# K slots in bundles of two, R's low channels in K's row-tile stretch: a convolution followed by a channel mix on one core

## The chip, the cores and the metric

The kernel runs on one core of a Trainium2 chip, alone. The metric is the device time of one execution in microseconds (us), the median of several runs. The engines are PE (TensorE, matmuls), PEld (its weight loads, which run beside the matmuls), DVE (VectorE), ACT (ScalarE), POOL (GpSimd) and SP (SyncE, which here only issues DMAs). PSUM, where matmuls write, has 8 banks of 512 float32 per partition.

## What is computed

Batch 8, sequence 4160, 192 channels, float32 in and out. First a causal convolution of 7 taps, with one softmaxed filter for each of 8 heads of 24 channels; then a channel mix on its result `y`:

```python
y  = conv(x, softmax(weight))                 # taps 0..6 back in time, per head
y1 = y shifted one step back in time
xk = mu_k * y + (1 - mu_k) * y1
xr = mu_r * y + (1 - mu_r) * y1
k  = relu(xk @ w_k)                           # 192 -> 1024
v  = (k * k) @ w_v                            # 1024 -> 192
out = sigmoid(xr @ w_r) * v                   # w_r: 192 x 192
```

## The kernel before

The work goes by **pairs** of batch rows ("sequences"), four in all. A pair is cut into **steps** of 512 positions (the first pair has 256, seven times 512, 256), and a tail of 64. A step of 512 has 8 **slots**; a slot is 128 of the 1024 K channels for both sequences, written to a PSUM tile of two banks (`psK`, two such tiles). 192 channels do not fit the 128 rows of the array, so each product over them is split: the *high* part contracts 128 channels, the *low* part the other 64. The low channels of sequence 0 lie on partitions 0 to 63 and those of sequence 1 on 64 to 127 (`xk[:, 2]`, `xr[:, 2]`), and K's low part is done as two matmuls of 64 rows (two row tiles), one for each half (`k_mm`, L343). Two slots form a bundle, in which PE does high, low, low, high: one stretch in row tiles for two slots.

After K: `k_relu` (ACT, L372) takes PSUM to `k_sb`, `k_square` (DVE, L391) squares it into `k2`. `v_mm` (PE, L433) makes 128 positions of one sequence from 8 matmuls over `k2`; `r_mm` makes the same 128 positions of R from a matmul over the high channels (L415) and one of the low channels (L416). L416 uses all 128 rows: the weights `wr[:, 2:4]` are padded with zeros where the other sequence's low channels lie. `r_sig` (ACT, L423) and `v_out` (DVE, L446) take two such tiles at once, and SP writes them out (L451).

Ahead of this runs the convolution. x is loaded by POOL's DMAs in **groups** of up to 10 blocks of 112 positions (`load_x`, L103 to L109, three buffers `xb`); `conv_mm` (PE, L199) multiplies by a banded matrix `toe`, in chunks of one to three heads; `conv_out` (ACT, L219 and L222) copies to `y`. `y` must then be transposed to have channels on partitions (`yT`). The first four groups do that on PE (`tr_mm` L257, `tr_out` on DVE L268); the others go through DRAM: `y_write` and `y_read`, a transposing DMA, both on SP (L234, L242). `diff` (DVE, L281) and `mix` (DVE, L301; four calls a step, for xk and xr, high channels 1024 wide and low channels 512 wide) make xk and xr from `yT`.

The order on each engine is the order in which the code calls: it is written out by hand. Tables `early`, `pe`, `act`, `dve` say which calls stand at which slot, relative to the first slot n0 of a step: `diff` at n0-7, the mixes at n0-5 to n0-2 (closer to the step for the first ones), R two slots ahead of its V, V from two slots after the step's last slot, `y_read` 17 slots (8.5 bundles) ahead of the step that needs it (11 slots in one group), the loads 14 slots before the group's convolution. A transposed pair of blocks is copied out one slot after its transposes. PSUM: `psK` 4 banks, `psV` 2 (V's results), `psM` 2 single banks, shared by convolution, transposes and R.

Of the kernel before, what the change touches and what calls it, by code (L numbers as in the profile page):

```python
# [14 lines left out]
def kernel(  # L15
# [29 lines left out]
    WARM = 34  # L45
# [7 lines left out]
    psM = ctx.enter_context(tc.tile_pool(name="psM", bufs=2, space=bass.MemoryType.PSUM))  # L53
# [4 lines left out]
    slots = []  # L58
    first_step = {}
    for p in range(NPAIR):  # L60
# [3 lines left out]
        for L in sizes + [TAIL]:  # L64
            ns = L * NF // STEP if L > TAIL else 1
            steps.append((p, t0, L, len(slots), ns))
            slots += [(len(steps) - 1, j) for j in range(ns)]
            t0 += L
    NSLOT = len(slots)
# [3 lines left out]
    for p in range(NPAIR):  # L73
        blk0 = 0
        for nb, s, on_pe in (
            ((3, 0, True), (4, 1, True), (5, 2, True), (4, 3, True), (10, 4, False), (6, 6, False), (6, 7, False))
# [59 lines left out]
    wr = const.tile([P, 4, D], BF16)  # L136
# [9 lines left out]
    def load_wr():  # L146
        nc.gpsimd.dma_start(out=wr[:, 0, :], in_=moe_w_r[0:P, :])
        for i in (1, 2):
            nc.gpsimd.dma_start(out=wr[0:LO, i, :], in_=moe_w_r[P:D, :])
        for i in (1, 3):  # L150
            nc.gpsimd.dma_start(out=wr[LO:P, i, :], in_=moe_w_r[P:D, :])
# [32 lines left out]
    ys, yTs, y_drams = {}, {}, {}  # L184
    conv_ps = {}
# [5 lines left out]
    def conv_mm(g, c, pool=None, tag="m"):  # L191
# [4 lines left out]
        ps = (pool or psM).tile([P, nb, 2, G * len(hs)], FP32, tag=tag, name="ps_c")  # L196
# [52 lines left out]
    def tr_mm(g, j):  # L249
# [3 lines left out]
        ps = psM.tile([P, 3, 2, BLK], BF16, tag="m", name="ps_t")  # L253
# [21 lines left out]
    def diff(s):  # L275
        p, t0, L, _, _ = steps[s]
        c0 = YC + t0
        d = two.tile([P, 3, STEP], BF16, tag="diff", name="d")
# [9 lines left out]
    def mix(s, i, part):  # L288
# [4 lines left out]
        if part == 0 and L > TAIL:  # L293
# [30 lines left out]
    def k_mm(n):  # L324


        s, j = slots[n]
        p, _, L, _, _ = steps[s]
        if L == TAIL:
            return k_mm_tail(n, p)  # L330
        xk = xks[s]
        ps = psK.tile([P, 2, BANK], FP32, tag="k", name="ps_k")
        k_ps[n] = ps
        first = j % 2 == 0
        nf = STEP // L


        def go(hi, start):
            for f in range(nf):
                fs = slice((j * nf + f) * P, (j * nf + f + 1) * P)  # L340
                for i in range(2):
                    r = slice(0, P) if hi else slice(i * LO, (i + 1) * LO)
                    nc.tensor.matmul(  # L343
                        out=ps[:, i, f * L : (f + 1) * L],
# [240 lines left out]
    with tc.manual_schedule():  # L585
# [4 lines left out]
        for ns in bundles():  # L590
            for n in ns:
                run(early, n)
# [41 lines left out]
```

## Time and profile before

| | |
|---|---|
| median of 3 runs | 469.6 us (469.21 to 470.67) |
| the profiled execution | 468.94 us, of which the span of the profile is 467.2 and 1.74 lie around it |
| granted PE clock, mean | 0.99 |
| PE busy | 445.2 us, 95% of the span |
| DVE busy | 390.4 us, 84% |
| ACT busy | 374.6 us, 80% |
| DMA | 65.79 MB, 141 GB/s on average |

The span runs from the first to the last instruction. A busy share is a mean over all stages, so it says which engine may be the bound, not that it is the bound everywhere; that is read from the timeline of each stage, and from which wait ends last there. Matmuls overlap in the pipeline: the duration of one (246 ns for 192 columns) is longer than the distance from one start to the next, and it is the distance that costs time.

### The profile page before, as it was taken

How to read it: one execution, taken by the hardware profiler on the slowest of the kernel's cores; microseconds unless marked ns; L12 is line 12 of the kernel's file. 1: busy time of each engine (PE TensorE's matmuls, PEld its weight loads, DVE VectorE, ACT ScalarE, POOL GpSimd, SP SyncE). 2: the span in 40 equal slices, each digit the busy share in tenths (PEclk: the TensorE clock that was granted, in tenths of full speed). 3: DMA queues.
4: the chain of work that ended last, by engine and by line, in shares of the span. 5: the costliest groups of instructions: out<-in, count | busy, mean ns of one | idle time of the engine just before them, and what ended most of it. 6: DMA issues, size and time to landing. Idle time of an engine off the chain costs nothing.

```text
span 467.2 us, 9868 instructions
## 1 busy us (share of the span) xinstructions
PE 445.2 (95%) x3892; PEld 300.6 (64%) x3954; DVE 390.4 (84%) x616; ACT 374.6 (80%) x549; POOL 51.1 (11%) x71
## 2 busy tenths in 40 slices
PE   7788999999999999999999999999999999999996
PEld 3454766666776666666676666666676666666676
DVE  2778988797998879889798989978898987999873
ACT  2489888988879797888879788888978888777771
POOL 5812211000010041000002041000002000000000
PEclk9799999999999999999999999999999999999999
DMA  7996699972459599945367679937157753511222
GB/s 89 160 174 106 162 197 156 233 200 68 127 142 183 148 139 229 181 129 139 93 173 119 165 133 214 229 100 187 52 152 138 173 135 100 153 65 56 69 69 94
DMA packets 138942, 65.79 MB, mean 141 GB/s; under 512 B 89936, under 2 KB 138464, under 8 KB 138896
## 3 DMA queue, kind: packets, MB, share of 16 engines
q1 hardware_dynamic: 98000, 49.26, 41.0%
q0 software_dynamic: 40896, 15.90, 30.0%
q8 instruction: 31, 0.51, 0.4%
q14 instruction: 15, 0.12, 0.1%
HBM read 31.59 MB, written 37.52 MB: 148 GB/s over the span
## 4 chain that ended last, share of the span: by engine, by line
PE 91%; ACT 2%; issue 2%; DMA 2%; DVE 1%; DVEq 0%; ACTq 0%
PE ps_k L343 38%; PE ps_v L433 37%; PE ps_c L199 5%; PE ps_r L416 5%; PE ps_r L415 5%; ACT k_sb L372 1%; DMA w_scr<-w_row 1%; PE ps_k L360 1%; DMA toe<-w_scr 1%; ACT y L219 1%; DMA w_raw<-in_weight_dram 1%; PE ps_t L257 1%; DVE yT L268 0%; ACT y L222 0%; DVE k L391 0%
## 5 line engine op out<-in xcount | busy, mean ns | idle before, releaser
L372 ACT ACTIVATE k_sb<-ps_k 128x1024 bf16<-128x1024 f32 x260 | 260.2, 1026 | 35.8 <-PE ps_k L343 31.8
L343 PE MATMUL ps_k<-xk,wk 64*128 64x512 bf16 (+2 forms) x994 | 206.0, 376 | 9.5 <-ACT k_sb L372 0.9
L433 PE MATMUL ps_v<-wv,k 128*128 128x192 bf16 x2048 | 210.8, 246 | 0.0
L433 PEld LDWEIGHTS <-k 128*128 128x128 bf16 x2048 | 175.4, 98 | 30.6 <-issue 1.4
L391 DVE TENSOR_TENSOR k<-k_sb 128x1024 bf16<-128x1024 bf16 x256 | 174.8, 684 | 16.7 <-ACT k_sb L372 16.0
L343 PEld LDWEIGHTS <-wk 64*128 64x128 bf16 (+1 forms) x1056 | 56.2, 96 | 109.2 <-issue 107.9
L446 DVE TENSOR_TENSOR o_sb<-ps_v,r_sb 128x384 f32<-128x384 f32 x132 | 72.2, 547 | 39.6 <-PE ps_v L433 34.7
L423 ACT ACTIVATE r_sb<-ps_r 128x384 bf16<-128x384 f32 x132 | 64.3, 487 | 38.1 <-PE ps_r L416 37.3
L301 DVE SCALAR_TENSOR_TENSOR xr<-d,mu,yT 128x1024 bf16<-128x1024 bf16 (+1 forms) x66 | 65.1, 988 | 0.1
L301 DVE SCALAR_TENSOR_TENSOR xk<-d,mu,yT 128x1024 bf16<-128x1024 bf16 (+1 forms) x66 | 64.4, 977 | 0.2
L415 PE MATMUL ps_r<-wr,xr 128*128 128x192 bf16 x256 | 62.8, 246 | 0.0
L416 PE MATMUL ps_r<-wr,xr 128*128 128x192 bf16 x256 | 62.8, 246 | 0.0
L219 ACT CAST y<-ps_c 112x480 bf16<-112x480 f32 (+4 forms) x100 | 47.9, 483 | 10.4 <-PE ps_c L199 10.2
L199 PE MATMUL ps_c<-xb,toe 128*112 128x480 bf16 (+5 forms) x152 | 46.2, 332 | 5.3 <-DMA toe<-w_scr 2.9
L109 POOL DMA_DIRECT2D xb<-in_x_dram x38 | 34.9, 928 | 26.8 <-PE ps_c L199 15.9
L281 DVE TENSOR_TENSOR d<-yT 128x1536 bf16<-128x1536 bf16 (+2 forms) x37 | 31.8, 859 | 0.4 <-DMA yT<-y_dram 0.2
L108 POOL DMA_DIRECT2D xb<-in_x_dram x8 | 4.3, 538 | 215.7 <-PE ps_k L343 206.3
L199 PEld LDWEIGHTS <-toe 128*112 128x112 bf16 x152 | 19.2, 134 | 12.1 <-DMA toe<-w_scr 3.4
L222 ACT CAST y<-ps_c 112x480 bf16<-112x480 f32 (+8 forms) x53 | 25.2, 482 | 0.2 <-DVE yT L227 0.2
L415 PEld LDWEIGHTS <-xr 128*128 128x128 bf16 x256 | 25.0, 98 | 0.0
L416 PEld LDWEIGHTS <-xr 128*128 128x128 bf16 x256 | 25.0, 98 | 0.0
L103 POOL DMA_DIRECT2D xb<-in_x_dram x8 | 4.6, 581 | 62.4 <-PE ps_r L416 61.0
(46 smaller groups left out, 67.8 us busy)
## 6 DMA issues: line engine op xcount, KB each, us to landing
out_dram<-o_sb SPq DMA_DIRECT2D x128, 192.0 KB, 2.3
y_dram<-y SPq DMA_DIRECT2D x7, 840.0 KB, 5.0
xb<-in_x_dram POOLq DMA_DIRECT2D x12, 432.0 KB, 12.0
y_dram<-y SPq DMA_DIRECT2D x6, 756.0 KB, 4.6
xb<-in_x_dram POOLq DMA_DIRECT2D x8, 480.0 KB, 13.2
xb<-in_x_dram POOLq DMA_DIRECT2D x6, 384.0 KB, 6.6
y_dram<-y SPq DMA_DIRECT2D x2, 504.0 KB, 10.7
xb<-in_x_dram POOLq DMA_DIRECT2D x4, 240.0 KB, 5.3
```

Source lines behind the costliest of these rows:

```text
L109: nc.gpsimd.dma_start(out=xb[:, lo:hi, s, :], in_=bass.AP(tensor=x.tensor, offset=x.offset + (b * S + t0 + lo * BLK) * D, ap=[[D, P], [BLK ...
L199: nc.tensor.matmul(out=ps[:BLK, :, :, i * G : (i + 1) * G], lhsT=toe[:, h, :], rhs=xbs[g][:, :nb, :, h * G : (h + 1) * G], start=True, sto ...
L219: copy(out=yh[:, :, :, c0 : c0 + n], in_=ps[:BLK, :, :, 0:n])
L301: nc.vector.scalar_tensor_tensor(out=o, in0=d[r0:r1, sl, :L], scalar=mu[r0:r1, i, part : part + 1], in1=yT[r0:r1, sl, c0 : c0 + L], op0=AL ...
L343: nc.tensor.matmul(out=ps[:, i, f * L : (f + 1) * L], lhsT=wk[r, 0 if hi else 1, fs], rhs=xk[r, i if hi else 2, :L], start=start and f == ...
L372: nc.scalar.activation(out=k_sb, in_=ps.rearrange("p a b -> p (a b)"), func=AF.Relu)
L391: nc.vector.tensor_tensor(out=o, in0=i, in1=i, op=ALU.mult)
L415: nc.tensor.matmul(out=o, lhsT=hi, rhs=wr[:, 0, :], start=True, stop=False)
L416: nc.tensor.matmul(out=o, lhsT=lo, rhs=wlo, start=False, stop=True)
L423: nc.scalar.activation(out=r_sb[:, :n, :], in_=ps[:, :n, :], func=AF.Sigmoid)
L433: nc.tensor.matmul(out=o, lhsT=k2[:, f, t * P : (t + 1) * P], rhs=wv[:, f, :], start=(f == 0), stop=(f == NF - 1),)
L446: nc.vector.tensor_tensor(out=o_sb[:, :n, :], in0=v_ps.pop(m)[:, :n, :], in1=r_sbs.pop(m)[:, :n, :], op=ALU.mult)
```

## The change

- A **bundle** is now the unit of every table: two K slots, and one V/R tile, which is 128 positions of *both* sequences. V's tile of a step starts in the bundle right behind the step's last one (before: one bundle further on).
- R's low part is done as K's: two matmuls of 64 rows, one for each sequence, in the same row-tile stretch as the two low parts of K. `wr` shrinks to two parts and its zeros go. R's PSUM tile takes two banks, one for each sequence, so `psM` is now one tile of two banks (`bufs=1`), which R and the convolution use in turn. Two convolution chunks can share the tile, a bank each.
- Transposes on PE now take `psV`'s banks, up to three behind each other in one bundle, each with its copy.
- In the first pair the groups are 3, 4, 5, 4, 5, 5 on PE and 5, 5, 2 through DRAM (before: 3, 4, 5, 4 on PE, and 10, 6, 6 through DRAM).
- The order within a bundle is fixed by the loop at the end. `diff` stands 5 bundles ahead of its step and the mixes at 4, 3, 2 and 1 (three buffers for `diff`); x is loaded 4 bundles before its convolution, `y_read` stands 3 bundles before the `diff` that needs it (2 in the first pair).
- 46 warm-up matmuls instead of 34.

```diff
-    WARM = 34
+    WARM = 46
-    psM = ctx.enter_context(tc.tile_pool(name="psM", bufs=2, space=bass.MemoryType.PSUM))
+    psM = ctx.enter_context(tc.tile_pool(name="psM", bufs=1, space=bass.MemoryType.PSUM))
...
+    tiles = []
+    for s, (p, t0, L, b0, nb) in enumerate(steps):
+        for c in range(max(1, L // P)):
+            tiles.append((s, c, max(b0 + nb, tiles[-1][2] + 1) if tiles else b0 + nb))
...
-            ((3, 0, True), (4, 1, True), (5, 2, True), (4, 3, True), (10, 4, False), (6, 6, False), (6, 7, False))
+            ((3, 0, True), (4, 1, True), (5, 2, True), (4, 3, True), (5, 4, True), (5, 5, True), (5, 6, False), (5, 7, False), (2, 8, False))
...
+    def m_banks():
+        shared[:] = [psM.tile([P, 2, BANK], FP32, tag="m", name="ps_m"), 2]
+        return shared[0]
+    def m_bank():
+        if shared[1] != 1:
+            m_banks()
+            shared[1] = 0
+        shared[1] += 1
+        return shared[0][:, shared[1] - 1, :]
...
-        ps = psM.tile([P, 3, 2, BLK], BF16, tag="m", name="ps_t")
+        ps = psV.tile([P, 3, 2, BLK], BF16, tag="v", name="ps_t")
...
-        d = two.tile([P, 3, STEP], BF16, tag="diff", name="d")
+        d = three.tile([P, 3, STEP], BF16, tag="diff", name="d")
...
+    def r_part(m, hi, start):
+        s, c, _ = tiles[m]
+        xr = xrs[s]
+        if start:
+            r_ps[m] = m_banks()
+        cs = slice(c * P, (c + 1) * P)
+        for i in range(2):
+            r = slice(0, P) if hi else slice(i * LO, (i + 1) * LO)
+            nc.tensor.matmul(
+                out=r_ps[m][:, i, :D],
+                lhsT=xr[r, i if hi else 2, cs],
+                rhs=wr[r, 0 if hi else 1, :],
+                start=start,
+                stop=not start,
+            )
...
+    START = {2: (0, 2), 3: (2, 2), 4: (4, 2), 5: (6, 1), 6: (9, 1), 7: (13, 1), 8: (18, 1)}
...
+        if p == 0:
+            c0, per = START[g]
         else:
...
+            c0, per = b0 - 18, 1
...
+            at(early, max(c0 - 4, 0), x_in, g)
...
+            at(side, c0 + c // per, conv, g, c, act_)
+        e = c0 + -(-nc_ // per)
...
+                at(side, e + j // 3, tr, g, j)
...
+            at(side, e - 1, y_write, g)
+            at(side, e + 2, y_read, g)
...
+        late = 3 if b0 == 2 else 2 if b0 == 6 else 0
+        at(mid, max(0, b0 - 5 + late), diff, s)
+        at(mid, max(0, b0 - 4 + late), mix, s, 0, 0)
+        at(mid, max(0, b0 - 3 + late) if b0 > 2 else 1, mix, s, 0, 1)
+        at(mid, b0 - 2 + (late > 0), mix, s, 1, 1)
+        at(mid, b0 - 1 + (late > 0), mix, s, 1, 0)
...
+            if slots == 2:
+                k_part(b, 0, True, True)
+                k_part(b, 0, False, False)
+                k_part(b, 1, False, True)
+            elif slots:
+                k_tail(b)
+            if m is not None and not r_in_full:
+                r_part(m, False, True)
+            if slots == 2:
+                k_part(b, 1, True, False)
+            if r_in_full:
+                r_tail(m)
+            elif m is not None:
+                r_part(m, True, False)
+            if slots:
+                k_relu(b, 0)
+            if m is not None:
+                r_sig(m)
+            if slots == 2:
+                k_relu(b, 1)
+            if m is not None:
+                v_mm(m)
+            if slots:
+                k_square(b, 0)
+            run(mid, b)
+            if slots == 2:
+                k_square(b, 1)
+            if m is not None:
+                v_out(m)
+            run(side, b)
```

`conv` is `conv_mm` and `conv_out` behind each other, `tr` is `tr_mm` and `tr_out`, `x_in` is `x_tile` and `load_x`; `k_part` is the body of `k_mm`'s `go`.

## The prediction

> **What bounds the kernel now.** I read the groups by line with their shapes first, then the timeline of a quiet stretch, then the first 50 us, then the DMA issues. The groups:
>
> ```profile
> L343 PE MATMUL ps_k<-xk,wk 128*128 128x512 bf16 x434 | 135.4, 382 | 0.6 <-issue 0.2
> L343 PE MATMUL ps_k<-xk,wk 64*128 64x512 bf16 x496 | 75.8, 381 | 8.8 <-ACT k_sb L372 0.9
> L415 PE MATMUL ps_r<-wr,xr 128*128 128x192 bf16 x256 | 62.8, 246 | 0.0
> L416 PE MATMUL ps_r<-wr,xr 128*128 128x192 bf16 x256 | 62.8, 246 | 0.0
> L281 DVE TENSOR_TENSOR d<-yT 128x1536 bf16<-128x1536 bf16 x31 | 29.6, 956 | 0.4 <-DMA yT<-y_dram 0.2
> ```
>
> PE has almost no idle time ahead of its groups (last column), and DVE hardly ever waits for a transposed yT (0.2 us in all). One bundle of the quiet stretch, 204.87 to 208.03:
>
> ```profile
> 204.87 1.67 PE L343 MATMUL ps_k<-xk,wk 128*128 128x512 bf16 x7
> 205.83 1.94 ACT L372 ACTIVATE k_sb<-ps_k 128x1024 bf16<-128x1024 f32 x2 [0.27 <-PE ps_k L343]
> 206.38 0.82 PE L433 MATMUL ps_v<-wv,k 128*128 128x192 bf16 x8
> 207.04 0.25 PE L415 MATMUL ps_r<-wr,xr 128*128 128x192 bf16 x1
> 207.12 0.25 PE L416 MATMUL ps_r<-wr,xr 128*128 128x192 bf16 x1
> 207.21 0.82 PE L433 MATMUL ps_v<-wv,k 128*128 128x192 bf16 x8
> 207.87 0.25 PE L415 MATMUL ps_r<-wr,xr 128*128 128x192 bf16 x1
> 207.95 0.25 PE L416 MATMUL ps_r<-wr,xr 128*128 128x192 bf16 x1
> 208.03 1.67 PE L343 MATMUL ps_k<-xk,wk 128*128 128x512 bf16 x8
> ```
>
> Starts follow each other without a gap: K 1.51, twice V 0.66 and twice R 0.165, together 3.16. A 192-column matmul costs 0.66/8 = 0.0825, so 512 columns cost 0.22. K's four high matmuls take 0.88, its four low ones 0.44 if the halves run side by side (0.88 if not, which would be over 1.51): 0.19 is left for two switches of row tiling, 0.095 each. **PE bounds all but the start.** The first 44 us are bound by chains through ACT, DVE and PSUM: bundle 7 (slots 14, 15) starts at 44.55, 25.3 after the first K at 19.26.
>
> **1. R's low part: a gain of 10.6.** Per bundle, two of four R matmuls become one pair side by side: 0.33 goes to 0.2475. There are 128 tiles of both sequences: 128 x 0.0825 = 10.6 us, all on PE's path. Nothing (the halves in turn) and 10.6 are the bounds; K's own pairs overlap, so I take 10.6. The stretch has one more pair but the same two switches; the two banks keep the halves apart. The padded weights' memset (0.22 on DVE at 2.06) and two DMAs (0.55 each on POOL) go for nothing: DVE waits then for w_raw (until 3.70), and nobody for x so early.
>
> **2. Stretches that were not there: +1.3.** Four tail bundles and three after the last K have R but no K pair: 7 x 0.19. [...]
>
> **3. The start: +3.5.** Engine queues are in order, so I lay the calls out by hand from rows: relu 1.02 (next start 0.92 later), square 0.61 from start to start, high mix 1.19, low mix 0.67, diff 0.89, v_out 0.47, conv copy 0.55, transposes of two blocks 0.28; K's first slot reaches ACT 0.96 after its start. In us after the first K:
> - Bundle 2's K needs xk of step 1. Its mixes now stand behind the squares of bundles 0 and 1: relu(1,0) ends at 4.76 behind two conv copies, square 4.8, high mix 5.4 to 6.7. K starts at 6.7, where before it was 5.1.
> - Bundle 2's V ends at 9.9. The second transpose wants V's bank, which v_out frees at 11.8, behind a mix and a square. Bundle 3 starts at 12.8, bundle 4 at 16.2, bundle 5 at 18.7.
> - Bundle 6: K's low part waits for its mix until 23.1, V's last matmuls for square(5,1) until 25.3, V ends at 26.1. DVE has two high mixes there (to 28.2), a square, v_out (29.35): the second transpose stands still for 3.0. Bundle 7 starts at 30.2.
>
> The 12 extra warm-up matmuls (12 x 0.22 = 2.6) end at 12.9, and `toe` lands at 13.19, so they cost nothing; before, the clock stood at half from 14.6 to 21.4 (granted clock 0.50), behind PE's idle time from 10.3 to 13.2, and if it stays full the first K comes up to 1 us sooner. I take 0.5: first K near 18.7 to 19.9, bundle 7 at 49.4 against 44.55, 4.9 later. Of that 1.4 comes back, since by then one V tile more (1.32) and five transposes' pairs more (0.7) are done, and 3.75 conv blocks (0.6) less. Bounds: 1.0 (half of the new waits absorbed) and 6 (the clock halved again in the gaps).
>
> **4. Transposes in bundle 10: +1.9, and +0.7 of work.** V ends at 3.1 in the bundle, v_out at 5.1 behind a mix of 1.19; the second transpose waits 1.6, the third 0.3. Ten more blocks with three transposes of 0.046 each: 1.4, of which half was counted above. Before, transposes stood one to a slot with their copies a slot later, and such waits came to 1.4 us in all:
>
> ```profile
> PE ps_c L199 <- DVE yT L268: 1.4, 4, 0.6
> ```
>
> **5. V right behind its step: +1.0.** In a step's last bundle DVE has square 2.02 to 2.63, mix to 3.8, diff to 4.7, second square until 5.4. The next bundle's V wants that square at its eighth matmul, at P + 2.25, P being the bundle: 5.54 with a conv chunk (P 3.29), 5.33 without (P 3.08). So 0.1 to 0.2 is lost in the last five steps, which have no conv beside them; were the estimate off by 0.2, all 32 steps would pay, 6 us. No more than one square (0.68 x 32) can come of it. DVE's whole load, 2.84 a bundle, stays under 3.08, and ACT's (0.92 + 0.45 + 0.92 + 0.48) too: neither becomes the bound by itself. R's tile waits for the conv copy in the one `psM` tile: copy ends at 4.05, R wants it at 4.26, so 0.2 is spare and I take 0.
>
> **6. yT later: +3.2.** This is the wait that is added. y_read stands behind the bundle's output DMA, so it is issued 4.65 to 4.95 into its bundle; the diff comes 3.8 into its own. Three bundles apart that leaves 8.7 us, two apart (first pair) 5.7. Three issues in the DMA view (the last number is the time from issue to landing):
>
> ```profile
> yT<-y_dram SPq DMA_TRANSPOSE x1, 5.7
> yT<-y_dram SPq DMA_TRANSPOSE x1, 13.5
> yT<-y_dram SPq DMA_TRANSPOSE x1, 10.8
> ```
>
> The first (issued at 50.56) had no x loads beside it, the others (67.10, 184.34) were issued while POOL's loads ran. Quiet ones take 5.3 to 6.7, loaded ones 8.7 to 13.5. Before, 10 us or more were left. Now: three reads of the first pair, each near the load of a later group, taken as landing in 6.3, 6.4 and 7.7 against 5.7 (waits of 0.6, 0.7, 2.0), and the last group's read in pairs 1 and 2, in the midst of the next pair's loads, taken as 9.4 against 8.7 (0.7 each): 4.7, less 0.3 that PE's order leaves spare at each of five = 3.2. Behind a waiting diff stand the bundle's second square and v_out, so the next V and PE wait as long. Bounds: 0 (all quiet) and 31 (five reads at 13.5: 3 x 7.8 + 2 x 4.8, less 1.5). x loads have room: 4 bundles and 3 us are 16, and a pair's first load needs some 2 until DVE's memset, 2 of issue and 8.6 to land (the one issued at 166.5).
>
> **7. The clock: +1.3.** PE now stands for 2 to 3 us at three places of the start. The one row for such a gap is the 2.9 us idle before 13.2, with 6.8 us at 0.50 clock soon behind it. Once more of that is worth 0 to 3.4 (half of 6.8, less what PE waits for anyway); I take 1.3, nearer to nothing, since the gaps of 1 us around 37 us left the clock at 1.00. [...]
>
> **Sum:** -10.6 + 1.3 + 3.5 + 1.9 + 0.7 + 1.0 + 3.2 + 1.3 = +2.3. Against the profiled 468.94 (span 467.2 and 1.74 around) that is 471.2; the median shown is 0.66 higher, so I expect a median of 471.9. About 0.3% (1.4 us) is what a measurement of this kernel can tell from no change.
>
> **Rivals.**
> - *The start does not suffer* (0.33): DVE is ahead in bundles 2, 6 and 10, so that v_out frees V's bank as soon as V ends. Price: 1.6 + 3.0 + 1.9 = 6.5 less, 465.4; **faster**. It decides from 3.7 us of these waits gone. For it: DVE idles 0.6 to 1.1 at a time from 28 to 35 us. Against: the copies stand behind the mixes in the same queue.
> - *yT reads land as loaded ones* (0.16): five diffs wait 2 us more each, +8 to 10: 481. For it: SP's reads stand nearer to the diffs; against: only two of the five surely meet the loads.
> - *The change doesn't do what it says* (0.06): R's pair does not overlap, or the one `psM` tile makes R wait in each bundle: 10.6 back, 482. Against: K's pairs, and 0.2 of slack.
> - *The sum as above* (0.45): 469 to 476 is its own range.
>
> **Numbers.** The likeliest is 471.9. Of the forecast's 0.45, 0.31 lie above 471.0, 0.11 within 0.3%, 0.03 below; of the first rival's, 0.28 below and 0.05 within; the others above. Faster 0.31, same 0.16, slower 0.53. The range takes in most of the first rival and the near half of the second: 464 to 481.
>
> **What would show it.** Right: quiet bundles without conv at 3.08 instead of 3.16, L416's line gone and a 64x192 group of R; bundle 7 near 49; idle PE ahead of transposes, put down to v_out; diffs waiting for yT. Wrong: bundle 7 before 46 (step 3), bundles still at 3.16 (step 1), waits ahead of V over 3 us in all (step 5), no wait for yT (step 6), granted clock 1.00 after 22 us (step 7).

## The result, and the profile after

The changed kernel took **490.5 us** (median of 4 runs, 484.4 to 493.6), the kernel before on the same chip 469.4 (469.0 to 470.7). The ratio is 1.036 with a 95% interval of 1.028 to 1.044; it is formed from undisturbed runs alone, and so lies under the quotient of the medians (1.045). A second measurement (`e0_changed_again` below) gave 488.6 and 1.042 (1.037 to 1.048). The prediction was 471.9 with a range of 464 to 481: the change makes the kernel slower by 17 us (the ratio) to 21 (the medians), where the upper end of the range allowed 12. The profiled execution took 492.5 us, of which the span is 490.7 (before: 467.2); the one profiled in the second measurement took 487.7, span 486.0.

**Where the change does what it says.** The groups by line and shape, after:

```profile
L358 PE MATMUL ps_k<-xk,wk 64*128 64x512 bf16 x496 | 76.8, 389 | 0.1
L415 PE MATMUL ps_m<-wr,xr 128*128 128x192 bf16 x256 | 42.8, 249 | 0.0
L415 PE MATMUL ps_m<-wr,xr 64*128 64x192 bf16 x256 | 32.1, 247 | 0.0
L300 DVE TENSOR_TENSOR d<-yT 128x1536 bf16<-128x1536 bf16 x31 | 29.6, 956 | 9.6 <-DMA yT<-y_dram 9.6
```

R's low part is now the 64x192 group, in place of the line L416 of before. Its busy time of 32.1 us against 62.8 overstates the gain, since matmuls overlap (one of V's lasts 247 ns, and below sixteen of them start within 1.32 us, 0.083 apart); the gain is read from the distances between starts. A quiet bundle, PE alone (start, duration, engine, line):

```profile
309.35 1.13 PE L358 MATMUL ps_k<-xk,wk 128*128 128x512 bf16 x6
310.32 0.25 PE L415 MATMUL ps_m<-wr,xr 64*128 64x192 bf16 x2
310.50 0.60 PE L358 MATMUL ps_k<-xk,wk 128*128 128x512 bf16 x2
310.94 0.33 PE L415 MATMUL ps_m<-wr,xr 128*128 128x192 bf16 x2
311.11 1.48 PE L445 MATMUL ps_v<-wv,k 128*128 128x192 bf16 x16
312.43 0.37 PE L218 MATMUL ps_m<-xb,toe 128*112 128x480 bf16 x1
```

The pair of 64x192 matmuls and the switch back take 0.18 (310.32 to 310.50), two high matmuls 0.17, and nothing has a bracket behind it, that is, nothing waits. Bundles without a convolution chunk take 3.07 to 3.08 (before 3.16), with one chunk 3.26 to 3.28 (before 3.36, and 3.52 to 3.60 with two).

**Where the time came from.** I take the start of each K bundle (its first weight load, some 0.1 to 0.2 ahead of its first matmul) in the profiled executions and sum by stretch (us); the last column is the second profile of the changed kernel against the same before:

| stretch | before | after | difference | second profile |
|---|---|---|---|---|
| up to bundle 21 | 92.2 | 108.9 | +16.8 | +14.3 |
| 21 to 53 | 105.7 | 104.0 | -1.6 | -1.6 |
| 53 to 56 | 10.1 | 15.1 | +5.0 | +4.9 |
| 56 to 86 | 99.1 | 97.5 | -1.6 | -1.8 |
| 86 to 89 | 10.1 | 18.3 | +8.1 | +6.2 |
| 89 to 131 | 136.0 | 133.4 | -2.6 | -2.6 |
| 131 to the end | 14.1 | 13.6 | -0.5 | -0.5 |

Starts are counted from bundle 0. Where a bundle of these later stretches is given a duration, it runs from the start of the bundle before it to its own start: what bundle 54 "takes" lies between the starts of 53 and 54.

So the quiet stretches gain 6.3 (6.5 in the second profile), and the start and two places near the change from one pair of rows to the next lose 29.9 (25.3). The view of waits names what is waited for (us in all, times, longest):

```profile
PE ps_v L445 <- DVE k L403: 10.0, 5, 5.5
DVE d L300 <- DMA yT<-y_dram: 9.6, 3, 5.7
PE ps_m L218 <- ACT y L241: 6.7, 8, 1.6
PE ps_t L276 <- DVE o_sb L458: 5.7, 3, 2.7
PE ps_m L218 <- ACT y L238: 4.6, 4, 1.6
```

Before, the waits of this kind were 1.4 us (convolution for a transpose's copy) and 0.2 us (diff for yT). The chain that ended last says the same in shares of the span:

```profile
PE 74%; DMA 10%; DVE 7%; ACT 4%; issue 2%; SPq 0%; DVEq 0%; ACTq 0%
```

Before, PE had 91% of this chain and DMA 2%.

**The start.** PE's timeline, only the lines with a wait (the bracket is the idle time ahead and what ended it) and two others:

```profile
41.76 0.36 PE L218 MATMUL ps_m<-xb,toe 128*112 128x240 bf16 x2 [0.93 <-ACT y L238]
...
45.42 0.36 PE L218 MATMUL ps_m<-xb,toe 128*112 128x240 bf16 x2 [1.58 <-ACT y L241]
...
48.69 0.46 PE L276 MATMUL ps_t<-ident,y 112*128 112x112 bf16 x6
51.84 0.72 PE L276 MATMUL ps_t<-ident,y 112*128 112x112 bf16 x9 [2.69 <-DVE o_sb L458]
...
52.61 1.73 PE L358 MATMUL ps_k<-xk,wk 128*128 128x512 bf16 x6
```

Two things stand out. Each second convolution chunk of a bundle waits for ACT to copy the first one out, though they have a bank each; over the first pair these waits come to 11.3 us (the two `ps_m` lines above). And the second transpose waits for V's bank, as predicted. Behind the gap of 2.69 us the same six K matmuls take 1.73 instead of 1.13: the granted clock is 0.50 from 52.9 to 56.3.

**The change of pair.** DVE, PE and SP around bundles 53 and 54:

```profile
205.99 9.48 SPq L261 DMA_TRANSPOSE yT<-y_dram  x1
...
214.93 0.74 PE L445 MATMUL ps_v<-wv,k 128*128 128x192 bf16 x7
...
217.52 0.96 DVE L300 TENSOR_TENSOR d<-yT 128x1536 bf16<-128x1536 bf16 x1 [3.72 <-DMA yT<-y_dram]
...
219.15 0.92 PE L445 MATMUL ps_v<-wv,k 128*128 128x192 bf16 x9 [3.48 <-DVE k L403]
...
220.10 1.97 PE L358 MATMUL ps_k<-xk,wk 128*128 128x512 bf16 x6
```

The write of y that this read needs, and the read, in the DMA view (the last number is the time from issue to landing):

```profile
y_dram<-y SPq DMA_DIRECT2D x1, 756.0 KB, 10.5
yT<-y_dram SPq DMA_TRANSPOSE x1, 11.5
```

The write is issued at 195.50 and lands at 205.95; the transposing read is issued at 205.99 and lands 11.5 us later, at 217.5. `diff` waits 3.72 for it; the second square stands behind `diff` in DVE's queue, so V's ninth matmul waits 3.48 in the midst of its product; and the K products after it run at half the clock (1.97 instead of 1.13; granted clock 0.51 from 220.2 to 223.6). At the next change of pair (bundle 87) the read is issued at 319.56, lands after 12.5, and the two waits are 5.74 and 5.49. Each such stop costs PE's wait and then 1.7 and 2.9 us of half clock: bundles 54 and 55 take 6.93 and 4.86, bundles 87 and 88 9.60 and 5.39, where 3.28 is the quiet value. POOL's timeline shows what is in flight meanwhile:

```profile
185.99 0.55 POOL L109 DMA_DIRECT2D xb<-in_x_dram  x1 [26.07 <-PE ps_m L415]
186.53 0.99 POOL L115 DMA_DIRECT2D xb<-in_x_dram  x1
187.52 0.56 POOL L109 DMA_DIRECT2D xb<-in_x_dram  x1
188.06 2.93 POOL L115 DMA_DIRECT2D xb<-in_x_dram  x3
194.18 1.98 POOL L115 DMA_DIRECT2D xb<-in_x_dram  x2 [3.19 <-PE ps_m L218]
```

L109 is the first load of a pair. It follows a memset on DVE (L97, done at 185.44), which the table puts into bundle 44 (the bracket names the matmul of R that ended last before the issue; `e11` below shows that the issue moves with the call); the loads of the next two groups stand behind it in POOL's queue though a buffer is free, and so three groups go out together, 10 us before and beside the y write (195.50, landed in 10.5) and its read.

### The profile page after: what moved, and what is told of

Same layout as the page of the kernel before. It is cut to its first block, busy times and chain, and to the rows that moved or that the text cites. A ratio compares the mean times of both kernels' runs of the same rounds, so it can differ in the third digit from the quotient of the medians.

```text
span 490.7 us, 10000 instructions
## 1 busy us (share of the span) xinstructions
PE 455.8 (93%) x4012; PEld 297.4 (61%) x4012; DVE 394.6 (80%) x621; ACT 384.0 (78%) x546; POOL 52.7 (11%) x73
## 4 chain that ended last, share of the span: by engine, by line
PE 74%; DMA 10%; DVE 7%; ACT 4%; issue 2%; SPq 0%; DVEq 0%; ACTq 0%
PE ps_k L358 32%; PE ps_v L445 29%; DMA yT<-y_dram 7%; PE ps_m L415 6%; PE ps_m L218 4%; DMA y_dram<-y 4%; DVE k L403 3%; ACT k_sb L385 3%; PE warm L554 2%; DVE xr L320 1%; DVE xk L320 1%; ACT y L238 1%; DVE o_sb L458 1%; DVE d L300 1%; ACT y L241 1%
## 5 line engine op out<-in xcount | busy, mean ns | idle before, releaser
L358 PE MATMUL ps_k<-xk,wk 64*128 64x512 bf16 (+2 forms) x1056 | 227.0, 382 | 0.2
L445 PE MATMUL ps_v<-wv,k 128*128 128x192 bf16 x2048 | 192.6, 247 | 10.1 <-DVE k L403 10.0
L445 PEld LDWEIGHTS <-k 128*128 128x128 bf16 x2048 | 171.9, 98 | 11.9 <-DVE k L403 11.4
L238 ACT CAST y<-ps_m 112x480 bf16<-112x480 f32 (+8 forms) x95 | 46.9, 494 | 42.9 <-PE ps_m L218 34.7
L415 PE MATMUL ps_m<-wr,xr 64*128 64x192 bf16 (+1 forms) x512 | 74.4, 248 | 0.0
L435 ACT ACTIVATE r_sb<-ps_m 128x384 bf16<-128x384 f32 x132 | 64.0, 485 | 8.0 <-PE ps_m L415 6.7
L415 PEld LDWEIGHTS <-xr 64*128 64x128 bf16 (+1 forms) x512 | 41.4, 97 | 46.3 <-issue 4.6
L320 DVE SCALAR_TENSOR_TENSOR xr<-d,mu,yT 128x512 bf16<-128x512 bf16 (+1 forms) x66 | 65.1, 988 | 0.0
L218 PE MATMUL ps_m<-xb,toe 128*112 128x432 bf16 (+5 forms) x161 | 45.4, 317 | 11.4 <-ACT y L241 6.7
L241 ACT CAST y<-ps_m 112x480 bf16<-112x480 f32 (+8 forms) x52 | 24.3, 467 | 6.5 <-PE ps_m L218 4.2
L554 PE MATMUL warm<-zeros,ones_t 128*128 128x512 bf16 x46 | 11.9, 426 | 1.4 <-DVE zeros L535 1.4
L109 POOL DMA_DIRECT2D xb<-in_x_dram x8 | 4.6, 577 | 78.2 <-PE ps_m L415 52.6
L276 PE MATMUL ps_t<-ident,y 112*128 112x112 bf16 x78 | 6.0, 212 | 7.1 <-DVE o_sb L458 5.7
```

What stands on the lines that cost most here:

```text
L218: nc.tensor.matmul(out=ps[:BLK, :, :, i * G : (i + 1) * G], lhsT=toe[:, h, :], rhs=xbs[g][:, :nb, :, h * G : (h + 1) * G], start=True, sto ...
L238: copy(out=yh[:, :, :, c0 : c0 + n], in_=ps[:BLK, :, :, 0:n])
L320: nc.vector.scalar_tensor_tensor(out=o, in0=d[r0:r1, sl, :L], scalar=mu[r0:r1, i, part : part + 1], in1=yT[r0:r1, sl, c0 : c0 + L], op0=AL ...
L358: nc.tensor.matmul(out=ps[:, i, f * L : (f + 1) * L], lhsT=wk[r, 0 if hi else 1, fs], rhs=xk[r, i if hi else 2, :L], start=start and f == ...
L415: nc.tensor.matmul(out=r_ps[m][:, i, :D], lhsT=xr[r, i if hi else 2, cs], rhs=wr[r, 0 if hi else 1, :], start=start, stop=not start,)
L435: nc.scalar.activation(out=r_sb[:, :n, :], in_=r_ps.pop(m)[:, :n, :D], func=AF.Sigmoid)
```

## The experiments

Two theories at the outset. **A**: the loss is three separate waits, each from an order or a distance that the change set: the second chunk behind the first one's copy, transposes behind `v_out`, and too little time between y's read and `diff` where x loads run; R's pair is a real gain that they hide. **B**: the new bundle itself is at fault (R's pair, or the one `psM` tile, costs what it saves), so undoing the orders brings little.

**Both chunks ahead of both copies.** `conv` is taken apart: the matmuls of a bundle's chunks first, the copies after them, then y's DMAs.

```diff
-            at(side, c0 + c // per, conv, g, c, act_)
+            at(side, c0 + c // per, conv_mm, g, c)
+            at(outs, c0 + c // per, conv_out, g, c, act_)
...
             run(side, b)
+            run(outs, b)
+            run(last, b)
```

> In a bundle with two convolution chunks both chunks' matmuls now stand ahead of both copies. Theory A (three separate waits on PE: second chunks behind the first chunk's copy, transposes behind v_out, and V behind a diff that waits for yT): the idle time ahead of second chunks in the trace of the changed kernel is 1.5 + 1.6 + 0.6 + 0.6 + 0.9 + 1.6 in bundles 0 to 5 and 0.7 + 0.7 + 0.7 + 1.6 + 0.6 + 0.4 later, 11.5 us in all, and goes; bundle 21 starts 8 to 11 us sooner (98 to 101 instead of 108.9), the time is 477 to 483. Theory B (these waits are a symptom: ACT and DVE are the bound there, so that PE waits elsewhere instead): bundle 21 moves by less than 3 us, the time stays at 484 to 492. A part must remain in either case, since K's next slots wait for the same copies in bundles 0 to 5.

Measured: 482.7 us, ratio 1.028 (1.024 to 1.032). Bundle 21 starts at 100.9 instead of 108.9 (106.4 in the second run of the changed kernel): 5.5 to 8.0 us off the start. PE's timeline has no wait ahead of a convolution chunk any more from 18 to 110 us. Part of it is given back in bundles 2 and 6, where K now waits for DVE's mixes:

```profile
25.19 0.39 PE L358 MATMUL ps_k<-xk,wk 128*128 128x512 bf16 x1 [2.29 <-DVE xk L320]
...
41.99 0.61 PE L358 MATMUL ps_k<-xk,wk 64*128 64x512 bf16 x4 [1.28 <-DVE xk L320]
```

Bundles 54 and 87 stay at 7.75 and 9.03. So this wait came from the order of the calls, not from PSUM's size, and it is one of three.

**Convolutions two bundles earlier.** 

```diff
-            c0, per = b0 - 18, 1
+            c0, per = b0 - 20, 1
```

> The convolutions of the pairs after the first stand two bundles further ahead (20 instead of 18 ahead of their step), with y_write and y_read. Theory A: the stops of 3.5 and 5.5 us at the start of bundles 54 and 87, and the half clock behind them, come from the chain y_write (10.5 and 11.5 us to land) and then y_read (11.5 and 12.5), which has 18 us and needs 22 to 24; with 24.5 us it fits: bundles 53 to 55 and 86 to 88 take 3.3 each, 11 to 13 us less, and two more bundles of the first pair have two chunks, 1.5 more: 479 to 483. Theory B (the transposing DMA is slow in the midst of the loads whenever it is issued and the loads move along with the convolution): the stops stay at 3 us or more, 486 to 492.

Measured: 488.0, ratio 1.040 (1.036 to 1.045), where theory A had 479 to 483. The stops at the change of pair are gone: bundles 54, 55, 87 and 88 take 3.28 each, though write (11.0 and 10.1 us) and read (10.3 and 10.0) land as late as before. That is 12 to 14 us gained against the two profiles of the changed kernel, and nearly all of it is lost again in the first pair, where the second pair's convolutions now meet the first one's. PE and ACT between the starts of bundles 22 and 23:

```profile
121.62 0.56 ACT L238 CAST y<-ps_m 112x480 bf16<-112x480 f32 x1 [4.79 <-DMA y_dram<-y]
122.23 0.26 PE L415 MATMUL ps_m<-wr,xr 64*128 64x192 bf16 x2 [4.35 <-ACT y L238]
```

The copy waits for a y write to free one of the y buffers, and R, which needs the one `psM` tile, waits for the copy. So the room matters, and the place where it is taken from matters as much.

**Transposes one to a bundle** (groups 4 and 5, as far as the blocks go, `j` in place of `j // 3`).

```diff
-                at(side, e + j // 3, tr, g, j)
+                at(side, e + (j if g > 3 else j // 3), tr, g, j)
```

> The transposes of groups 4 and 5 stand one block pair to a bundle instead of three in one. Theory A: the waits of 2.7 (bundle 6) and 1.5 us (bundle 10) for the V bank that v_out frees go, 4.2 us, and with the first of them the half clock from 52.9 to 56.3 (1.7 at most): 3 to 6 us less, 482 to 488. Theory B: DVE is behind in these bundles in any case, so that V's wait for the last square grows instead; less than 1.5 us.

Measured: 485.8, ratio 1.036 (1.034 to 1.038). Bundle 11 starts at 64.7 instead of 70.7 (68.4 in the second run), and bundle 21 at 103.1: 3.3 to 5.8 us. The 2.69 us ahead of the transposes of bundle 6 are gone with the second set of three there. The second of the three waits is shown.

**R's low part over full rows again**, padded weights, behind the high parts: the one part that was to bring the gain, undone.

```diff
-    wr = const.tile([P, 2, D], BF16)
+    wr = const.tile([P, 4, D], BF16)
...
-                lhsT=xr[r, i if hi else 2, cs],
-                rhs=wr[r, 0 if hi else 1, :],
+                lhsT=xr[:, i if hi else 2, cs],
+                rhs=wr[:, 0 if hi else 2 + i, :],
...
-                r_part(m, True, False)
+                r_part(m, True, True)
+                r_part(m, False, False)
```

> R's low part is again done over all 128 rows with padded weights, behind K's and R's high part; everything else as changed. Theory A: the row-tile pair saves 0.083 us in each of 125 bundles and costs 0.19 in seven without K: without it +8.5 to +9.5 where PE is the bound, less what waits take up in the first pair (1 to 2): bundles at the end go from 3.08 to 3.16, the time is 492 to 500. Theory B (the pair does not run side by side, or PE is not the bound in the steady stretches): no change beyond 2 us, bundles at the end stay at 3.08.

Measured: 492.3, ratio 1.049 (1.045 to 1.054). Bundles take 3.36 instead of 3.28 with a chunk and 3.16 instead of 3.07 without: 0.08 to 0.09 each. In PE's timeline R's four full matmuls, from their start to V's, stand 0.33 apart:

```profile
309.44 0.49 PE L416 MATMUL ps_m<-wr,xr 128*128 128x192 bf16 x4
309.77 1.48 PE L446 MATMUL ps_v<-wv,k 128*128 128x192 bf16 x16
```

In three stretches without stops (bundles 24 to 53, 55 to 86, 89 to 131) it is 1.9, 2.0 and 3.0 us slower than the changed kernel. The totals hide this, since the stop at bundle 87 is shorter here (6.30 instead of 9.60). Theory B falls with this run: the shared stretch gains in every bundle of these stretches.

**y's read two bundles earlier**, and nothing else.

```diff
-            at(side, e + 2, y_read, g)
+            at(side, e, y_read, g)
```

> Only y_read stands two bundles earlier than in the changed kernel, y_write where it was. The prediction's step 6 had the read's place in the program set its issue: then bundles 54 and 87 lose 5 us of waiting between them, 481 to 486. Theory A as it stands now (the write lands 10.5 to 11.5 us after its issue in the midst of the loads, and the read is issued at that moment, so that its place is not what delays it): bundle 54 and 87 change by less than 0.7 each, the time stays at 484 to 493, and out DMAs queue behind the read.

Measured: 484.2, ratio 1.031 (1.025 to 1.036), which lies in both ranges; the bundles decide. At bundle 54 nothing comes of it (7.25): SP's queue has the write at 194.93, its landing takes 10.6, and the read, called two bundles earlier, still goes out at the same moment:

```profile
194.93 0.42 SPq L253 DMA_DIRECT2D y_dram<-y  x1
205.50 8.30 SPq L261 DMA_TRANSPOSE yT<-y_dram  x1
```

205.50 less 194.93 is the write's landing time: the read waits for its data. At bundle 87 the expectation missed: 5.15 instead of 8.95 to 9.60, because the read, issued again at the moment of the write's landing (318.22), took 9.0 instead of 12.5. Why it landed sooner there is not shown. At the first place an earlier call is worth nothing as long as the write is late too; the whole chain from convolution to read has to move.

**The changed kernel once more.**

> The changed kernel once more, as the measure for the other three on this chip: 484 to 493 in every theory.

Measured: 488.6, ratio 1.042 (1.037 to 1.048). Writes land in 10.4 and 11.5, reads in 11.4 and 11.8, bundles 54 and 87 take 6.87 and 8.95. Bundle 21 starts at 106.4, 2.5 earlier than in the other profile; 1.6 of it is a half-clock window at 52.9 which this run has not, behind the same gap (2.68 us ahead of the transposes), most of the rest (0.75) is there by bundle 7.

**Three orders together:** chunks ahead of copies, transposes spread, and the convolutions two bundles earlier only in the third and fourth pairs and the second pair's last group.

```diff
-            c0, per = b0 - 18, 1
+            c0, per = b0 - (20 if p > 1 or blk0 == 29 else 18), 1
```

> All three waits taken away together: both chunks' matmuls ahead of their copies, the transposes of groups 4 and 5 one block pair to a bundle, and the convolutions of the last group of the second pair and of all later pairs 20 bundles ahead instead of 18 (no shift of the groups that overlap the first pair, which in the run with all groups shifted held the copies behind y_write for 4.8 us). Theory A (three waits, each its own price): bundle 21 near 96 (8 us by the chunks, 5 to 6 by the transposes, 2 of which overlap, from 108.9), bundles 54 and 87 at 3.3, and so 490.7 - 11 - 12 = 466 to 470, level with the kernel before. Theory B (the waits share one cause, DVE being late in the first pair): not below 474.

Measured: 472.0, ratio 1.007 (1.004 to 1.009), between the two expectations. Bundle 21 starts at 96.6, and bundles 54, 55, 87 and 88 take 3.28. A new stop stands at bundle 38 (7.72, then 4.64): the shifted group's loads now go out from 139.4 to 142.5, right ahead of another group's read (issued at 142.13, landed after 10.8). No other x load is in flight there: one group is enough to make a read late.

**Mixes ahead of the squares in the first seven bundles**, added to that.

```diff
+            if b < 7:
+                run(mid, b)
             if slots:
                 k_square(b, 0)
-            run(mid, b)
+            if b >= 7:
+                run(mid, b)
```

> As the run before, and in bundles 0 to 6 the differences and mixes stand ahead of the bundle's first square on DVE. Theory A: what is left in the start is K waiting for xk (1.3 and 2.3 us at bundles 2 and 6) behind squares which themselves wait for relu: 2 to 4 us less than the run before, 463 to 467, bundle 7 at 41 to 43. Theory B: the squares come later instead and V waits for them; within 1 us.

Measured: 470.2, ratio 1.001 (0.999 to 1.004), so no difference from before that can be told. Bundle 7 starts at 42.4, 2.6 earlier than in the run above. The stop at 38 stays (8.13, then 4.06); the read there was issued at 139.90, among that group's loads, issued from 137.2 to 140.2, and lands after 10.8:

```profile
150.71 0.96 DVE L300 TENSOR_TENSOR d<-yT 128x1536 bf16<-128x1536 bf16 x1 [3.16 <-DMA yT<-y_dram]
...
152.33 1.62 PE L445 MATMUL ps_v<-wv,k 128*128 128x192 bf16 x9 [3.51 <-DVE k L403]
```

**That one load two bundles earlier**, added again.

```diff
-            at(early, max(c0 - 4, 0), x_in, g)
+            at(early, max(c0 - (6 if p == 1 and blk0 == 29 else 4), 0), x_in, g)
```

> The kernel of the run before (both chunks' matmuls ahead of the copies, one block pair of transposes per bundle, mixes ahead of the squares in the first seven bundles, convolutions two bundles earlier in the second and third pairs of steps) with one more edit: the group whose convolution moved into the end of the first pair has its x load six bundles ahead of it instead of four, at bundle 31 instead of 33. There the load was issued at 137.2 to 140.2 us and the y read of the same bundle at 139.9; bundles 38 and 39 took 8.1 and 4.1 us. Theory A (transfers that are in flight together land late, and the stop at 38 is this one meeting): bundles 38 and 39 go back to about 3.9 and 3.3, the kernel comes to 463 to 465 us, about 1% under the kernel before. Rival B (the load now meets the y write of bundle 30 and delays that instead, or the stop has another cause): a stop of 3 us or more at some bundle from 35 to 40 again, 468 to 471.

Measured: **465.4, ratio 0.992 (0.990 to 0.994)**, the version that beats both kernels. The stop at 38 is gone (4.04, then 3.68), and the clock is 1.00 from start to end, but for the drain. All 37 diffs together wait 1.0 us for yT:

```profile
L300 DVE TENSOR_TENSOR d<-yT 128x1536 bf16<-128x1536 bf16 (+2 forms) x37 | 31.8, 859 | 1.1 <-DMA yT<-y_dram 1.0
```

What did the work is room, not faster transfers. The read that feeds bundle 54 still takes 11.2 us here, by the DMA view of its issue at 189.16:

```profile
yT<-y_dram SPq DMA_TRANSPOSE x1, 11.2
```

Its `diff` starts at 201.43, 12.3 us after the issue, and waits for nothing.

**The same with R's low part over full rows** (the edit of `e5_r_full`).

> The same as e9_load_early, with R's low channels over all 128 rows again (padded weights, behind the high parts), as in e5_r_full, so without the shared row-tile stretch of V and R's low channels. Theory A (the shared stretch is worth about 0.083 us in each bundle, which the stops of the changed kernel hid in its total): slower than e9_load_early by 8 to 9 us after the seven extra stretches at 0.19 each are taken off, about 472. Rival B (what the stretch gives is taken back at each change of row tiles, or other waits fill it): less than 2 us between the two.

Measured: 471.1, ratio 1.005 (1.003 to 1.006): 5.7 us slower than the version above, not 8 to 9. From bundle 53 to 131 it loses 5.6, and 0.5 comes back in the drain, where the extra stretches go. Up to bundle 53 it loses nothing: it is 0.8 ahead there, of which 0.7 is an earlier first K. Bundles without a wait take 3.36 against 3.28 there too, but the shorter ones only reach the next wait earlier (bundles 17 to 21 and bundle 46, where it is the version above that stands longer): chains through ACT, DVE and the DMAs set the time. (Between the two profiled executions the difference is 4.3, or 5.0 from the first K on.) So the shared stretch alone turns 0.5% slower into 0.8% faster, once the orders are mended.

**The head of the clump of loads five bundles earlier**, alone, in the changed kernel.

```diff
-            at(early, max(c0 - 4, 0), x_in, g)
+            at(early, max(c0 - (9 if p > 1 and blk0 == 0 else 4), 0), x_in, g)
```

> The changed kernel with one edit: the first x load of the third and fourth pairs of rows stands 9 instead of 4 bundles ahead of its convolution. In the changed kernel that load waits for a small memset on DVE in bundle 44, and the two groups behind it, whose buffers are free by then or soon, wait behind it in POOL's queue: all three go out between 186.0 and 196.2 us, around the y write at 195.5 (landed 10.5 us later) and ahead of its read at 206.0 (landed in 11.5); the same again from 298.6 to 308.7. With the edit the first two go out near 168 to 172, and only the third stands near the write. Theory A (the clump of loads makes write and read late, and so the stops at bundles 54, 55, 87 and 88): write in at most 7 us, read issued at its place and landed in 5 to 8, the four bundles at 3.3 to 3.9, 11 to 13 us off the changed kernel's time, 476 to 478; the write of the group before, at 169.5, may take 10, which its read has room for. Rival B (the last group's write and read are slow for a reason of their own, or the loads stop another write instead): bundles 54 and 87 still 6 us or more, or new stops of that size near 46 and 79, and 484 or more.

Measured: 494.3, ratio 1.053 (1.052 to 1.055): the total went the other way. The stops at 54, 55, 87 and 88 are gone (3.28 each), as A had it, and new ones stand at 46 and 79 (10.03 and 10.83), as B had it. They moved by exactly the eight bundles that lie between one group and the next:

```profile
179.81 9.33 SPq L261 DMA_TRANSPOSE yT<-y_dram  x1
...
193.69 0.96 DVE L300 TENSOR_TENSOR d<-yT 128x1536 bf16<-128x1536 bf16 x1 [6.16 <-DMA yT<-y_dram]
```

The loads of two groups went out from 169.4 to 174.4; the write of 169.1 was ahead of them and landed in 5.2, and the read of 179.81, 5 us behind the last load's issue, took 13.9. So the loads are the cause of the late landing. What I had wrong is how long they are in the way: the loads themselves took up to 19.3 us to land, and the room I had counted for the write was needed by the read.

**The same edit in the best version**, in place of the two bundles' shift.

```diff
-            c0, per = b0 - (20 if p > 1 or blk0 == 29 else 18), 1
+            c0, per = b0 - 18, 1
...
-            at(early, max(c0 - (6 if p == 1 and blk0 == 29 else 4), 0), x_in, g)
+            at(early, max(c0 - (9 if p > 1 and blk0 == 0 else 4), 0), x_in, g)
```

> The kernel of e9_load_early, but with the convolutions of all later pairs back at their places in the changed kernel (18 bundles ahead of the step) and, in place of that shift, the edit of e11_loads_apart. If the clump of loads is the cause, this does the same as the shift of two bundles: no bundle from 34 to 131 over 4 us, bundles 38 and 39 at 3.9 and 3.3, and 463 to 466, about the time of e9_load_early. If the shift was needed for another reason, stops of 3 us or more come back at bundles 54 and 87, and it is 470 or more.

Measured: 481.1, ratio 1.025 (1.024 to 1.027): missed in the same way, with bundles 46 and 79 at 8.43 and 10.60, and 54 and 87 at 3.28.

**One group out of the clump, at one place.**

```diff
-            at(early, max(c0 - 4, 0), x_in, g)
+            at(early, max(c0 - (22 if p == 2 and blk0 == 0 else 4), 0), x_in, g)
```

> The changed kernel with one edit: the first x load of the third pair of rows stands 22 instead of 4 bundles ahead of its convolution, at bundle 26, where its buffer has just come free and no other load is out. The load behind it then goes out when its own buffer is free, near bundle 39, and the third near bundle 56, so that the three no longer go out together; the next pair's loads are left as they were. Theory A (the clump fills the DMA engines, and the read that falls into it is late; the kernel before had the same clump but 10 us more of room): bundles 54 and 55 at 3.3 (6.9 and 4.9 in the changed kernel), write at 195 landed in 5 to 6 instead of 10.5 and its read in 5 to 7 instead of 11.5, no stop of 3 us from bundle 34 to 60; bundles 87 and 88 still at 9 to 9.6 and 4 to 5.4. In all 5 us less than the changed kernel, 483 to 486. Rival B (one load near a read is enough): a stop of 3 us or more near bundle 30, 46 or 54 again, and 487 or more.

Measured: 488.4, ratio 1.032 (1.023 to 1.040), which can't be told from the changed kernel. Bundles 54 and 55 take 3.28 each, as A said, and 87 and 88 stay at 8.06 and 4.43 (A: 9 to 9.6 and 4 to 5.4); the read lands in 7.4 instead of 11.5. But the write lands in 10.0, not in 5 to 6, and the load that was moved met a read again: two groups went out together from 128.8 to 133.9 (I had counted one), the read of 128.46 took 8.6, and bundles 31 and 32 took 5.43 and 4.86. So A holds for the reads at both changes of pair, and B at bundle 31: two groups' loads beside a read are enough where the read has 6.7 us of room (128.46 to 135.20). For the write one group right ahead of it is enough. The write at 199.47 has only the two loads of one group beside it (issued at 198.14 and 199.12), and so has the one at 173.42, which takes 10.3, and the one at 203.41 in `e11`, which takes 9.9:

```profile
xb<-in_x_dram POOLq DMA_DIRECT2D x2, 432.0 KB, 9.1
y_dram<-y SPq DMA_DIRECT2D x1, 756.0 KB, 10.0
```

What the clump adds is loads that are still in flight when the read follows (the last lands at 215.53 in the changed kernel, at 210.60 here).

## Why the prediction was wrong

The direction was the likelier one of the three; the size was not. By its steps:

**1, R's low part (-10.6): right per bundle, too large in sum.** The 0.0825 per tile was measured as 0.08 to 0.09. But I multiplied it by all 128 tiles, also those up to bundle 53, where waits for ACT, DVE and the DMAs take the gain back; with step 2's seven stretches the net was to be -9.3 and was measured as -5.7 (`e9` against `e10`), all of it behind bundle 53.

**2, the extra stretches (+1.3): right.** The drain is 0.53 longer with them (13.13 against 12.60) for the three that lie there, 0.18 each.

**3, the start (+3.5): this step failed by leaving a wait out.** Bundle 7 was to start at 49.4 and started at 52.5 (51.8 in the repeat). I had laid out DVE's queue by hand and found the transposes' waits, but let a bundle's two chunks follow each other freely, because the change gives them a bank each. They are one tile with two copies, and the second chunk's matmuls, called after the first one's copy, wait for it: 11.3 us in all, 5.5 to 8.0 at bundle 21. With only this order changed, bundle 7 starts at 48.9 (`e1`), and the waits for the mixes at bundles 2 and 6 that I had laid out are there (2.29 and 1.28). (My own numbers, a first K 0.5 earlier and 30.2 from there, make 49.0 and not 49.4.) I had looked at this tile in step 1's rival and in step 5, but only for R against the copy, with one chunk to a bundle.

**4, the transposes (+1.9 and +0.7): right as a mechanism**, put down to `v_out` as foreseen: 1.49 at bundle 2, 2.69 at 6 and 1.49 at 10, where I had 1.6, 3.0 and 1.9.

**5, V right behind its step (+1.0): about nothing.** Of PE's 10.0 us of waits for `k`, the two stops hold 8.97; the other three waits make 1.0 in all. A step's change costs 0.03 (3.11 instead of 3.08).

**6, yT later (+3.2): the wait was foreseen, its size and places were wrong, and the chain behind it was cut short by a link, the write; this step failed most, and put the time outside the range together with step 3.** Three reads of the first pair were to wait 0.6, 0.7 and 2.0; their landings of 4.3 to 5.8 us cost nothing to speak of. The two reads at the changes of pair were to land in 9.4 and wait 0.7 each; they landed in 11.5 and 12.5, their diffs waited 3.72 and 5.74, and with the half clock behind each they cost 5.0 and 8.1. Three things were mis-sized. I chose 9.4 between rows of 8.7, 10.8 and 13.5 that I had myself quoted for loaded reads. I had the read issued 4.65 to 4.95 us into its bundle, where it is 6.1 (199.87 to 205.99) and 7.1, which leaves 7.8 and 6.8 us and not 8.7. And I had not asked whether the write is loaded too: it took 10.5 and 11.5, and both reads went out within 0.04 us of its landing, so that an earlier call cannot bring the first one forward (`e8`). The trace before had shown it: its writes at 175.04 and 284.28 took 9.2 and 10.4, and the reads went out 0.1 us behind the landing. It had the same loads and landings of 10.8 and 8.7 there, but 14.7 and 13.5 us from issue to `diff`, so 3.9 and 4.9 to spare. (Nor did every read have 10 us or more before: the one at 50.56 had 5.7, and its `diff` waited 0.2.)

**7, the clock (+1.3): right in kind, too small.** The first profile has half-clock windows (granted clock 0.50 to 0.51) of 3.4 us at 32.4, 52.9 and 220.2 and one of 6.8 at 332.8, none of which before had (it had one of 6.8 at 14.6, which is gone, and the first K starts 0.9 sooner; in the other profiles of the new order, 0.0 to 1.2). One window costs about 1.6 (bundle 55: 4.86 less 3.28). I had weighed only the start, not the stops that step 6 would bring. The 3.48 and 5.49 of the stops in the first profile were followed by half the clock, from 220.2 and 332.8 on; in the second, stops of 3.42 and 4.84 lost 4.9 and 6.2 in all. A gap of 2.69 us was followed by it in one run, and one of 2.68 was not in the other, so the length of a gap did not settle it alone.

**The rivals.** "yT reads land as loaded ones" was the right cause with five waits of 2 us in place of two of 4 and 6. "The change doesn't do what it says" named the one `psM` tile as the danger, but for R in each bundle; it came for the convolution in the first pair. What was not on the list was that the stop of DVE for yT also halves PE's clock behind it (1.00 before the two stops, 0.51 from 220.2 on and 0.50 from 332.8).

**How it adds up.** The prediction against its own profile was 471.2; the two profiled executions of the changed kernel took 492.5 and 487.7, 21.3 and 16.5 more. The stops at the changes of pair have 13.1 and 11.1, where I had 1.4 less 0.6 of slack: 12.3 and 10.3 too little. Chunks behind copies are 8.0 and 5.5. Gain taken too large is 3.6. These make 23.9 and 19.4. The other way go what I had counted and what did not come: 2.4 for the first pair's reads in step 6, and 1.0 in step 5. That leaves 20.5 and 16.0, within 1 us of both. The parts come from different kernels, so this is an account and not a proof.

What stays open: how the DMA engines share their time between the queues (beside the loads the output's DMAs are slow too, 5.7 to 8.9 us from 189.8 to 205.5 in the changed kernel, where those from 230 to 240 take 1.9), and how far a group's loads must stand from a write or a read. To let loads out one group at a time is not enough by itself: in `e6` and `e7` a single group, right ahead of a read, made it land in 10.8 and brought the stop at bundle 38. No kernel here held a load back by anything but a free buffer and the order on POOL's queue.

## What to carry to other kernels

When a tile is made larger so that two producers have a bank each, write down the order of calls as well: matmul, copy, matmul, copy on one tile was a chain here (11.3 us of waits), and both matmuls ahead of both copies was not (none from 18 to 110 us in `e1`). When a transfer's lead is cut, price it with the slowest landing that the trace before shows for that stage, for every link of its chain (write and read), and look who else is on the DMA engines then; a lead that looks idle may be the cover. A saving per bundle was worth its price only in the bundles which that engine bounds (5.6 us from bundle 53 to 131, nothing before), so subtract the stretches that chains set before multiplying.

## What the runs showed of the hardware

- A y write of 756 KB landed in 4.7 us with no load beside it (issued at 169.46), in 10.5 with three groups of x loads in flight (195.50), and in 9.9 to 10.4 with one group issued right ahead of it (`e11`, `e13`). Transposing reads of 756 or 840 KB took 5.3 to 7.0 us in the changed kernel with no load beside them (issued at 292.69 and 239.83), 11.5 and 12.5 behind the clump, 13.9 and 14.7 in `e11`, and 10.8 right behind a single group (`e7`). In the loaded stretch the core's DMA engines moved 231 GB/s, in a quiet one of the same kernel 145 GB/s (last column; the one before is the DMA share, the first the window):

```profile
196.00:206.00 10.00, 10.00 (x93) 6.68 (x91) 9.44 (x14) 8.69 (x13) 0.16 (x1) 1.00 1.34 231
...
230.00:240.00 10.00, 10.00 (x92) 6.63 (x91) 9.09 (x13) 9.04 (x13) 0.00 (x0) 1.00 0.48 145
```

- The stop of PE of 3.48 us cost 5.2 in all (bundles 54 and 55 took 6.93 and 4.86, where 3.28 is the quiet value), since half the clock followed it for 3.4 us. Behind the gap of 2.69 us half the clock began when PE was back at work:

```profile
49.10:51.80 2.70, 0.05 (x2) 0.00 (x0) 2.70 (x5) 0.00 (x0) 0.00 (x0) 1.00 0.97 108
...
52.90:56.30 3.40, 3.40 (x17) 1.55 (x16) 1.47 (x3) 1.97 (x4) 0.00 (x0) 0.50 0.12 40
```

  PE's busy time is the second number, the granted clock the third from the end: 1.00 in the gap, 0.50 from a microsecond after it on. That microsecond is no constant: in the stop of 5.49 us half the clock began at 332.79, before PE was back at 333.72.
- The length of a gap did not decide it alone. Behind the gap of 2.69 us (49.15 to 51.84) in the first profile the granted clock was 0.50 from 52.90 to 56.30, and six K matmuls took 1.73 us; behind the gap of 2.68 (48.41 to 51.09) in the second profile five took 0.92, the pace of full clock (six in 1.13). The window at 32.4 stands behind gaps of only 1.49 and 0.57 us. What else decides was not shown.
